# Reordering the first transfers of a retention-plus-MLP kernel: token chunks ahead of weight pieces, refills held back, more dummy matmuls

## The chip, the cores and the metric

The kernel runs on one core of one Trainium2 chip. The time is the device time of one execution in microseconds (us), the median of several executions. The profile is one execution recorded by the hardware profiler. Its engines are PE (TensorE matmul), PEld (its weight loads), DVE (VectorE), ACT (ScalarE), POOL (GpSimd) and SP (SyncE, which here issues transfers). L331 is line 331 of the kernel that was profiled, and the change and each experiment shift the lines a little: the scaling of a chunk is L331 before and L346 after. "PEclk" is the share of full speed that TensorE's clock was granted. In the profile's lines `kq` is a chunk's k and q, `am` its masked scores, and `r`, `hp` and `o` hold results of matmuls; the brackets give the engine's idle time before the line and what ended it.

## The reference

A retention layer (a linear attention with decay) is followed by an MLP with the activation h * erf(softplus(h)).

```python
for t in range(S):                                   # B=4, H=8, S=768, D=64
    state = gamma * state + k[t] (outer) v[t]
    y[t] = scale * q[t] @ state
x = y.transpose(0, 2, 1, 3).reshape(3072, 512)
h = x @ w_in                                         # 512 x 2048
out = (h * erf(softplus(h))) @ w_out                 # 2048 x 512
```

q, k and v are float32; the weights arrive as float64.

## The kernel before

The tokens are worked on in 24 chunks of 128. Chunk j needs k, q and v (256 KB each, three places in a ring of buffers). VectorE scales k and q (`K_`), TensorE transposes them (`T`), makes scores (`S_`), VectorE masks (`M`), TensorE makes outputs (`O_`) and the state's update (`U`), and VectorE adds the update to the state (`A`). The weights arrive in 16 pieces of 1 MB, p0 to p15, of which p0 to p3 are of w_in ("in") and p4, p5 of w_out ("out"). Each is read as raw 64-bit words into one of four spare places and turned into float32 by six VectorE steps and one on ScalarE (`conversion`). These steps are generators, taken one at a time by `pace`, so that they fall between the other instructions of VectorE. When a piece is converted its place is free, and the next piece for that place is loaded.

```python
def load(j):                                   # chunk j: k, q, v
    ...
    for i, src in enumerate((k, q)):
        queue = nc.scalar if i and j < 3 else nc.sync
        queue.dma_start(KQ[j][:, i], ...)
    nc.sync.dma_start(V[j], ...)

def load_pieces_after(n):                      # piece n is converted: refill its place
    for later in range(n + 1, n_p):
        if place[later] == place[n]:
            load_piece(later)
            break
...
load(0)
...
load_piece(0)
load(1)
load_piece(1)
load(2)
...
for _ in range(10):
    nc.tensor.matmul(idle, ident, ident, start=True, stop=True)
...
def ret_state(j):                              # U
    ...
    if j + 3 < NJ:
        load(j + 3)
    if j < 2:
        load_piece(j + 2)
...
for j in range(6):                             # the first six chunks, before any MLP work
    S_(j); M(j); K_(j + 1); O_(j)
    if j + 1 < 6: T(j + 1)
    U(j); pace(1)
    if j + 1 < 6: A(j)
# then hidden(0, u), u = 0..3, with chunks 6 and 7 between:
#   T(6) after u=0;  K_(7) within u=1;  S_(6), T(7) after u=1;  M(6) within u=2; ...
```

## Time and profile before

| | kernel before |
|---|---|
| median time (first three runs) | 758.63 us (758.58 to 760.79) |
| span of the profiled run | 756.3 us |
| TensorE busy | 96% |
| start of unbroken matmuls | 87.2 us |
| transfers moved from 0 to 63.46 us | 212 GB/s at a DMA share of 1.04 |

The head, some 87 us, is where TensorE waits; the remaining 669 us are matmuls back to back. The prediction below shows and reads the lines.

### The profile page before, as it was taken

The page shows a single profiled execution, that of the slowest core. Times are in us where ns is not written, and L with a number is a line of the kernel's source. Part 1 is how long each engine was busy: PE and PEld are TensorE (multiplying, and loading weights), DVE is VectorE, ACT ScalarE, POOL GpSimd, SP SyncE. Part 2 cuts the span into 40 slices and gives each one's busy share as a digit, 9 for nine tenths or more (in the row PEclk, how much of TensorE's full clock was granted, in tenths as well). Part 3 has the DMA queues.
Part 4 walks back from the last instruction along what each step waited for, and adds up shares of the span by engine and source line. Part 5 has one row for each costly group of instructions (what it writes and reads, how often), then busy time and mean ns, then how long its engine had stood idle before and what let it go on. Part 6 is the DMA issues. An engine that isn't in the chain of part 4 may idle for free.

```text
span 756.3 us, 11745 instructions
## 1 busy us (share of the span) xinstructions
PE 726.7 (96%) x5236; PEld 611.5 (81%) x5236; DVE 353.3 (47%) x463; ACT 274.8 (36%) x320; POOL 31.9 (4%) x28
## 2 busy tenths in 40 slices
PE   6857999999999999999999999999999999999997
PEld 5644444447699999999999999999999999999995
DVE  3759899985463243243153053163163152153323
ACT  2313663441524424414424424324234244324430
POOL 1000200000110110110100110101100000000000
PEclk7879999999999999999999999999999999999999
DMA  9996754202120220220220230220200000000000
GB/s 190 207 246 147 186 131 145 101 0 40 59 42 2 42 70 1 43 71 1 43 70 1 43 70 1 42 60 11 44 29 1 1 29 1 1 29 1 1 28 29
DMA packets 87522, 42.71 MB, mean 56 GB/s; under 512 B 76208, under 2 KB 76208, under 8 KB 87472
## 3 DMA queue, kind: packets, MB, share of 16 engines
q1 hardware_dynamic: 83920, 41.16, 22.9%
q10 hardware_dynamic: 3552, 0.80, 0.7%
q8 instruction: 41, 0.67, 0.4%
q14 instruction: 9, 0.07, 0.0%
HBM read 35.66 MB, written 6.29 MB: 55 GB/s over the span
## 4 chain that ended last, share of the span: by engine, by line
PE 89%; DMA 4%; DVE 3%; ACT 1%; SPq 1%; issue 1%; DVEq 0%; ACTq 0%
PE hp L536 33%; PE o L596 31%; PE o L479 7%; PE hp L466 6%; DMA kq<-in_q_dram 3%; PE r L340 2%; PE r L393 2%; PE r L353 2%; PE r L407 2%; PE r L388 1%; DMA w_in_sb<-in_moe_w_in_dram 1%; PE hp L353 1%; DVE am L365 1%; DVE kq L331 0%; DMA kq<-in_k_dram 0%
## 5 line engine op out<-in xcount | busy, mean ns | idle before, releaser
L536 PE MATMUL hp<-xs,w_in_sb 128*128 128x128 f32 x1280 | 158.7, 278 | 0.0
L536 PEld LDWEIGHTS hp<-xs,w_in_sb 128*128 128x128 f32 x1280 | 150.3, 192 | 6.7 <-issue 3.2
L596 PE MATMUL o<-w_out_sb,h 128*128 128x256 f32 x640 | 141.6, 379 | 0.0
L455 DVE TENSOR_TENSOR e<-h,e 128x1024 f32<-128x1024 f32 x44 | 51.9, 1222 | 180.1 <-ACT e L436 180.1
L596 PEld LDWEIGHTS o<-w_out_sb,h 128*128 128x128 f32 x640 | 121.6, 190 | 16.5
L536 PE MATMUL hp<-xT,w_in_sb 128*128 128x128 f32 x960 | 113.7, 275 | 0.0
L536 PEld LDWEIGHTS hp<-xT,w_in_sb 128*128 128x128 f32 x960 | 111.9, 192 | 1.9 <-issue 1.0
L596 PE MATMUL o<-w_out_sb,e 128*128 128x256 f32 x480 | 111.5, 382 | 0.9 <-DVE e L455 0.9
L596 PEld LDWEIGHTS o<-w_out_sb,e 128*128 128x128 f32 x480 | 88.1, 190 | 12.5 <-DVE e L455 1.3
L435 ACT ACT_TABLE_LOAD x24 | 30.8, 1283 | 91.1 <-PE o L596 89.1
L466 PE MATMUL hp<-xT,w_in_sb 128*128 128x512 f32 x128 | 56.9, 599 | 0.0
L564 DVE TENSOR_TENSOR h<-h,hp 128x512 f32<-128x512 f32 x20 | 13.8, 688 | 86.7 <-PE hp L536 86.7
L331 POOL TENSOR_TENSOR kq<-kq,kq_s 128x1024 f32<-128x1024 f32 x15 | 29.7, 1981 | 501.7 <-DMA kq<-in_q_dram 429.0
L466 PEld LDWEIGHTS hp<-xT,w_in_sb 128*128 128x128 f32 x128 | 24.2, 193 | 28.9 <-issue 28.2
L559 DVE TENSOR_TENSOR h<-h,hp 128x512 f32<-128x512 f32 x20 | 13.8, 688 | 71.1 <-ACT h L557 71.1
L436 ACT ACTIVATE e<-e 128x2048 f32<-128x2048 f32 x22 | 42.1, 1913 | 0.2
L435 ACT ACTIVATE e<-h 128x2048 f32<-128x2048 f32 x22 | 42.1, 1912 | 0.2
L398 ACT COPY xT<-r 128x256 f32<-128x256 f32 x42 | 13.9, 376 | 75.7 <-PE r L393 75.7
L340 PE MATMUL r<-ident,kq 128*128 128x128 f32 x168 | 24.7, 291 | 14.3 <-DVE kq L331 9.9
L562 ACT COPY h<-hp 128x512 f32<-128x512 f32 x20 | 11.7, 587 | 70.8 <-PE hp L536 70.8
L365 DVE TENSOR_TENSOR am<-r,causal 128x512 f32<-128x512 f32 x42 | 27.2, 684 | 15.8 <-PE r L353 15.8
L340 PEld LDWEIGHTS r<-ident,kq 128*128 128x128 f32 x168 | 20.6, 151 | 16.0 <-issue 9.4
(91 smaller groups left out, 688.6 us busy)
## 6 DMA issues: line engine op xcount, KB each, us to landing
w_out_sb<-in_moe_w_out_dram SPq DMA_DIRECT2D x14, 512.0 KB, 4.6
kq<-in_k_dram SPq DMA_DIRECT2D x24, 256.0 KB, 3.3
v<-in_v_dram SPq DMA_DIRECT2D x24, 256.0 KB, 4.3
w_in_sb<-in_moe_w_in_dram SPq DMA_DIRECT2D x12, 512.0 KB, 6.8
out_dram<-r SPq DMA_DIRECT2D x24, 256.0 KB, 2.3
kq<-in_q_dram SPq DMA_DIRECT2D x21, 256.0 KB, 4.1
w_out_sb<-in_moe_w_in_dram SPq DMA_DIRECT2D x4, 512.0 KB, 10.1
w_in_sb<-in_moe_w_out_dram SPq DMA_DIRECT2D x2, 512.0 KB, 4.0
```

What stands on the lines that cost most here:

```text
L331: engine.tensor_tensor(KQ[j], KQ[j], by, op=ALU.mult)
L340: nc.tensor.transpose(p[:, u, :], KQ[j][:, i, 2 * u : 2 * u + 2, :].rearrange("p h d -> p (h d)"), ident,)
L353: nc.tensor.matmul(pp[s][:, hp, :], KT[j][s * D : (s + 1) * D, hp, :], QT[j][s * D : (s + 1) * D, hp, :], start=True, stop=True,)
L365: nc.vector.tensor_tensor(AM[j][:, s], SC[j][s], causal[:, None, :].to_broadcast([P, HP, C]), op=ALU.mult)
L393: nc.tensor.matmul(place(h), V[j][:, h, :], AM[j][:, h % 2, h // 2, :], start=(not c and h % 4 < 2), stop=True, skip_group_check=True,)
L435: nc.scalar.activation(E[g], HS[g], AF.Softplus)
L436: nc.scalar.activation(E[g], E[g], AF.Erf)
L455: nc.vector.tensor_tensor(E[g][:, half], HS[g][:, half], E[g][:, half], op=ALU.mult)
L466: nc.tensor.matmul(p, w_in_of(ft, kk), XC[0][:, kk, :], start=(kk == 0), stop=(kk == n_k - 1))
L479: nc.tensor.matmul(O[0][tt].rearrange("p (d c) -> p d c", d=2), E[g][:, u * TCH + tt * P : u * TCH + (tt + 1) * P], w_out_of(ft), start=(f ...
L536: nc.tensor.matmul(bank[:, u, :], w_in_sb[:, s, IN[a], kk, u * P : (u + 1) * P], XS[m][b][:, kk, :], start=(p in (1, 2, 5) and u == 0 and ...
L596: nc.tensor.matmul(O[m][i][:, half, :], G[g][a][:, u * P : (u + 1) * P], w_out_sb[:, s, OUT[b], u, :], start=i not in started, stop=(s == ...
```

## The change

The intent is to let chunks of tokens, for which TensorE waits, arrive ahead of weights for which nothing waits yet, and to keep TensorE's clock up with dummy matmuls in the first gaps. The core of the diff:

```diff
     def load_pieces_after(n):
         for later in range(n + 1, n_p):
             if place[later] == place[n]:
-                load_piece(later)
+                if early:
+                    held.append(later)
+                else:
+                    load_piece(later)
                 break
+    def load_held():
+        for n in held:
+            load_piece(n)
+        held.clear()
...
+    load(1)
     load_piece(0)
-    load(1)
+    load(2)
     load_piece(1)
-    load(2)
...
-    for _ in range(10):
-        nc.tensor.matmul(idle, ident, ident, start=True, stop=True)
+    def keep_warm(n):
+        for _ in range(n):
+            nc.tensor.matmul(idle, ident, ident, start=True, stop=True)
+    keep_warm(16)
...
+        if j >= 4:
+            load_held()
         if j + 3 < NJ:
             load(j + 3)
-        if j < 2:
-            load_piece(j + 2)
+        if j in (1, 2):
+            load_piece(j + 1)
...
     T(0)
+    keep_warm(3)
...
         S_(j)
+        if j == 0:
+            keep_warm(3)
...
     early = False
+    load_held()
```

More of the change, by code (lines that the diff above doesn't have):

```diff
@@ L151, in load_piece @@
                 )
+    held = []
     def load_pieces_after(n):
```

## The prediction

> **What bounds the kernel now.** I read the page's slices first, to see where the TensorE (PE) is not full.
>
> ```profile
> PE   6857999999999999999999999999999999999997
> DVE  3759899985463243243153053163163152153323
> ...
> PEclk7879999999999999999999999999999999999999
> DMA  9996754202120220220220230220200000000000
> GB/s 190 207 246 147 186 131 145 101 0 40 59 42 2 42 70 1 43 71 1 43 70 1 43 70 1 42 60 11 44 29 1 1 29 1 1 29 1 1 28 29
> ```
>
> A slice is 756.3 / 40 = 18.9 us. PE is short of nine tenths in the first four slices only, some 76 us, and there the transfers are near full. Then the chain of work that ended last, in order of time: from 87.26 us on it holds matmuls almost without a break.
>
> ```profile
> 38.05 10.89 DMA kq<-in_q_dram
> 48.93 0.03 issue
> ...
> 78.58 0.71 PE r L407 x16
> ...
> 87.26 13.93 PE hp L466 x32
> 101.19 13.73 PE o L479 x32
> ```
>
> So the run is a head of 87.26 us and 756.3 - 87.26 = 669.0 us of matmuls. Nothing in the diff removes one of those, so I predict the head alone. What PE waits for there is in the timeline by engine (start, duration, instruction, in brackets the idle time before it and its releaser):
>
> ```profile
> 50.35 1.09 PE L340 MATMUL r<-ident,kq 128*128 128x128 f32 x4 [6.57 <-DVE kq L331]
> ...
> 70.78 1.97 PE L340 MATMUL r<-ident,kq 128*128 128x128 f32 x8 [4.14 <-DVE am L365]
> ```
>
> ```profile
> 49.03 1.23 DVE L331 TENSOR_TENSOR kq<-kq,kq_s 128x1024 f32<-128x1024 f32 x1 [6.18 <-DMA kq<-in_q_dram]
> ...
> 64.65 1.22 DVE L331 TENSOR_TENSOR kq<-kq,kq_s 128x1024 f32<-128x1024 f32 x1
> ```
>
> I call chunk j of k, q and v "c j", weight piece n "p n", and the VectorE (DVE) scaling of chunk j (L331) "K j". K5 idled 6.18 us for c5's q, K1 2.03 us for c1's q, K2 1.43 us for c2's k. The long PE gap at 66.6 to 70.8 us is different: T(7) waits for a mask multiply that stands behind weight conversions on DVE. Why c5 came late, the issues of the SyncE queue show:
>
> ```profile
> 33.44 1.76 SPq L138 DMA_DIRECT2D w_in_sb<-in_moe_w_in_dram  x2
> 35.29 2.20 SPq L146 DMA_DIRECT2D w_out_sb<-in_moe_w_out_dram  x2
> 37.59 0.41 SPq L95 DMA_DIRECT2D kq<-in_k_dram  x1
> 38.05 4.29 SPq L95 DMA_DIRECT2D kq<-in_q_dram  x1
> ```
>
> p3 (L138) and p4 (L146), 2 MiB together, stand ahead of c5. Yet the first conversion step of p4 ran on DVE only at 64.05 us. The windows confirm that the transfers are the limit up to about 63 us: 0.00 to 63.46 us moved 212 GB/s at a DMA share of 1.04, and only 46 to 48 us was nearly empty (85 GB/s).
>
> **What the Trainium skill says.** "DMA: Bandwidth & Descriptors", section "Issuing engines are not separate DMA queues": transfers issued from different engines run on the same 16 DMA engines and interleave. The trace agrees: c1's q, issued from ScalarE at 4.28 us, landed 10.66 us later beside p0 from SyncE, where c0's q took 4.6. So order decides, not the queue. The same page, "Why small descriptors are slow (HBM only)": a 256-byte descriptor pays a 27% overhead in the engine. The chunks move in packets of 256 bytes here; a chunk (0.79 MB) landed every 3.0 to 3.3 us, that is about 250 GB/s, while an "out" piece reached about 350 GB/s. "TensorE: Matmul & The Clock Gate", Part 1: the clock is halved by default and released after a busy window of some 3.4 us. The trace agrees: the granted clock is 0.50 from 8.6 to 22.3 us, and again from 46.2 to 56.4 and 70.1 to 73.5 us after idle stretches, the changes being multiples of 3.41 us apart. The same page, "Architectural detail": DVE is strict first-in, first-out. The trace shows DVE idle before K5 with later conversion steps of landed pieces behind it.
>
> **The change, part by part.** Bytes are unchanged up to c8; the order is not. Before: c0 p0 c1 p1 c2 c3 p2 c4 p3 p4 c5 c6 p5 c7 c8. After: c0 c1 p0 c2 p1 c3 c4 p2 c5 p3 c6 p4 p5 c7 c8. Ahead of c5, p3 and p4 go away; ahead of c6, p4; ahead of c7, nothing.
>
> Service times, from landings in the trace: chunk 3.2 us (c6 3.29, c7 2.98, c8 3.13); "in" piece 5.2 us (p2: 28.38 to 33.70); "out" piece 2.8 us (p4: 44.73 to 47.25; p5 3.96). Starting at c0's 6.4 us, the new order adds up to c1 9.6, p0 14.8, c2 18.0, p1 23.2, c3 26.4, c4 29.6, p2 34.8, c5 38.0, p3 43.2, c6 46.4, p4 49.2, p5 52.0, c7 55.2 us. The old order gives the same 55.2 us for c7, but the trace shows 60.33, so 5.1 us are lost to interleaving of two queues early and to the hole at 46 to 48 us. I let half of it return, in proportion: c5 39.6, c6 48.4, c7 57.7 us. q lands about 0.8 us ahead of v.
>
> DVE, with the spacings of the kernel before as cost. K1 starts at about 12 us, after the masks of chunk 0, instead of 15.06. The next DVE steps are p0's first conversion steps, and p0 is now later than c1: I take 16.0 us. Their 2.6 us (0.69 + 1.22 + 0.69), the state copy (0.42) and two masks (1.27) put K2 at 20.2, before 24.14. K3 follows by the old 6.87 at 27.1; K4 by 5.56 at 32.6; K5 by 6.26 (old K4 to the end of the masks of chunk 4) at 38.9, its q having landed at 38.8. K5 gains 49.03 - 38.9 = 10.1 us. K6 would follow by 7.56 at 46.5, but its q lands at 47.6: K6 47.7, before 56.59, gain 8.9. K7 follows by 8.06 at 55.8, but its q lands at 56.9: K7 57.0, before 64.65. The gain has shrunk to 7.6 us, since c7 has as many bytes ahead of it as ever.
>
> From K7 to T(7) DVE does the same steps (6.13 us), so T(7) moves from 70.78 to 63.1. From there on PE, ScalarE and DVE hand over to each other. The PE gap before T(7) grows, since PE reaches it earlier than DVE does: chunk 6's scores would end at about 56. The clock is then surely halved at T(7), and for longer than the 2.7 us of before. T(7) took 1.97 us at half speed against 1.04 for T(6); I charge 1.2 us more for this stage (an estimate: half of one further 2.4 us at half clock). Net: 7.6 - 1.2 = 6.4 us.
>
> Dummy matmuls: the first ten took 4.30 us; six more at 0.22 to 0.43 us are 1.3 to 2.6 us, ending by 6.8 to 8.3, where T(0) starts at 7.28. Three more fill the 0.73 us gap before S(0), and three the 1.31 us before O(0). They cost about nothing, at worst 1 us at T(0). They may save 1 us each on S(0), T(1), S(1), which the wait for p0 swallows. I count zero.
>
> 758.63 - 6.4 = 752.2 us.
>
> **The rivals.** First, full return: c6 and c7 land at the ideal times and DVE alone paces. DVE was busy 35.8 us between K1 and K7 (23.26 + 4.68 + 7.84, windows 15.06:49.03, 49.03:56.59, 56.59:64.65). From 12 us, with some 4 us of hand-over idling, K7 comes at 52 to 53: gain 11 to 12, less the clock, 748. Against it: c7 would need every byte ahead of it at undisturbed rates. Second, transfer-bound throughout: c7 lands at 60.3 as before. K7 at 59.7, gain 5, less the clock, 755. For it: the loaded bytes are the same, and the long issues (4.29 us) show a full queue. Third, p0 becomes the stall: with q2 interleaved it lands at 18 us, DVE stands on it and K2 gains nothing. The later chunks still gain from their order, so 753 to 756. Fourth, the held pieces starve conversions: p4 would have to land after about 57 us (K7's new time), p5 after about 65. I expect both by 55, so this is worth nothing. Beyond 87 us PE is full and every refill is released by a conversion, which moves along.
>
> **Range and chances.** The first and second rivals bound it at 748 and 755; the reported runs differ among themselves by 2 us. I take 749 to 756. Over 2% would be 15.2 us, more than DVE's own work in the head allows; slower by 2% would need a new stall of 15 us beyond the gain. So 0.98 for within 2%.
>
> **What would show it.** In the new timeline: the idle before K5 gone and K5 near 39; K6 and K7 waiting for q, if at all, by about 1 us; T(7) near 63 with a PE gap of over 6 us; p4 and p5 landed before their first steps; unbroken matmuls from about 81 us. A wait of DVE L176 on p0 near 14 to 16 us would be new. The prediction is wrong if c7 lands at 60 or later, if the matmuls after 87 us take other than 669 us, or if the clock stays full through the T(7) gap.

## The result, and the profile after

The changed kernel takes 754.58 us (median of four runs, 754.10 to 756.00); the kernel before took 759.39 us in the same rounds. The ratio is 0.9938 (95% interval 0.9916 to 0.9960). All ratios here are the mean time of one kernel's runs over that of the other's runs of the same rounds, so not quite the ratio of the medians quoted. Executions over 1.5% slower than the fastest of the same kernel are left out of the means. In five later rounds the same kernel came out at 0.9939. That is within 2%, and within the predicted range of 749 to 756 us, though 2.4 us above the predicted 752.2.

The page of the changed kernel, its 40 slices (18.8 us each now):

```profile
PE   7884999999999999999999999999999999999997
...
PEclk9997999999999999999999999999999999999999
DMA  9999755102120120120220220120200000000000
```

TensorE is still short in the first four slices. The first three together have more TensorE work than before (7, 8, 8 against 6, 8, 5), the fourth has less (4 against 7): the waiting moved to a later place. The transfers are full to the end of the fourth slice. VectorE's timeline, the scalings K5, K6 and K7 in order:

```profile
39.77 1.23 DVE L346 TENSOR_TENSOR kq<-kq,kq_s 128x1024 f32<-128x1024 f32 x1 [0.77 <-DMA kq<-in_q_dram]
...
49.93 1.22 DVE L346 TENSOR_TENSOR kq<-kq,kq_s 128x1024 f32<-128x1024 f32 x1 [3.23 <-DMA kq<-in_q_dram]
...
60.10 1.23 DVE L346 TENSOR_TENSOR kq<-kq,kq_s 128x1024 f32<-128x1024 f32 x1 [2.04 <-DMA kq<-in_q_dram]
```

The 6.18 us of idle time ahead of K5 are down to 0.77, but K6 and K7, which waited for no transfer before, now wait 3.23 and 2.04 us for theirs. K5 is 9.26 us earlier than before, K6 6.66 (it stood at 56.59), K7 4.55. The landing of c7 caps the gain. TensorE's timeline from T(7) on:

```profile
66.24 1.97 PE L355 MATMUL r<-ident,kq 128*128 128x128 f32 x8 [9.39 <-DVE am L380]
68.00 5.46 PE L483 MATMUL hp<-xT,w_in_sb 128*128 128x512 f32 x8
...
84.03 14.00 PE L483 MATMUL hp<-xT,w_in_sb 128*128 128x512 f32 x32
```

The same stretch of the kernel before, whose first line (70.78) and whose 87 us stand in the prediction, has this for the second:

```profile
72.54 4.08 PE L466 MATMUL hp<-xT,w_in_sb 128*128 128x512 f32 x8
```

T(7) came 4.54 us earlier, but its followers took longer, at a clock of 0.50 from 61.5 to 71.8 us. Unbroken matmuls start at 84.03, 3.16 us earlier than before (87.19 in the same view). After them nothing changed: 752.8 - 84.03 = 668.8 us, before 669.1. The chain that ended last, in order of time (start, duration, what), carries the transfer:

```profile
47.63 3.65 PE hp L483 x8
51.27 0.06 SPq L95
51.33 0.04 issue
51.38 8.63 DMA kq<-in_q_dram
60.01 0.03 issue
60.06 0.04 issue
60.10 1.23 DVE kq L346
```

From 51.38 to 60.01 us the end of the whole run hangs on c7's q; before, it hung on c5's q, from 38.05 to 48.93 us. (The step to TensorE just before is inferred by the profile and is not read here: SyncE issued p5 until 50.37 us and c7's k from 50.48 to 51.33, without a stop.) The profiled runs differ by 3.5 us (756.3 and 752.8), the timed ones by 4.8: the kernel before ran between 757 and 762 us over all rounds, and its profiled run (758.04) is on the quick side.

### The profile page after: what moved, and what is told of

It is laid out like the page before. It is cut to its first block, busy times and chain, and to the rows that moved or that the text cites. A ratio compares the mean times of both kernels' runs of the same rounds, so it can differ in the third digit from the quotient of the medians.

```text
span 752.8 us, 11796 instructions
## 1 busy us (share of the span) xinstructions
PE 726.2 (96%) x5260; PEld 610.7 (81%) x5260; DVE 353.2 (47%) x463; ACT 274.5 (36%) x320; POOL 32.2 (4%) x28
## 4 chain that ended last, share of the span: by engine, by line
PE 90%; DVE 4%; DMA 2%; ACT 1%; issue 1%; SPq 1%; ACTq 0%; DVEq 0%
PE hp L553 34%; PE o L613 32%; PE o L496 7%; PE hp L483 7%; PE r L408 2%; PE r L355 2%; PE r L368 2%; PE r L422 1%; DMA w_out_sb<-in_moe_w_in_dram 1%; DMA kq<-in_q_dram 1%; PE r L403 1%; DVE am L380 1%; DVE w_out_sb L191 0%; SPq L96 0%; DVE w_out_sb L201 0%
```

## The experiments

Twelve kernels ran, the two that are compared among them; every experiment's output was correct. Theory 1: K7 now waits for c7, which has the same bytes ahead of it as before the change; everything that happens to earlier chunks is hidden under that. Theory 2: VectorE's own chain bounds K7, so the order of the early chunks is what counts. Theory 3: the clock after the idle gap before T(7) takes back a part. The table has for each profiled run when c7's q landed, when K7 and T(7) began and when the unbroken matmuls began (us), then the time in rounds.

| run | c7's q | K7 | T(7) | unbroken | median | ratio (95%) |
|---|---|---|---|---|---|---|
| before | 59.46 | 64.65 | 70.78 | 87.19 | 758.6 to 759.4 | 1 |
| changed | 60.01 | 60.10 | 66.24 | 84.03 | 754.58 | 0.9938 (0.9916-0.9960) |
| after_again | 60.71 | 60.80 | 66.94 | 84.66 | 753.87 | 0.9939 (0.9920-0.9959) |
| b1_behind_c7 | 52.94 | 58.65 | 64.78 | 81.39 | 752.14 | 0.9914 (0.9901-0.9928) |
| c1_warm_gap | 60.42 | 60.52 | 66.66 | 81.94 | 751.84 | 0.9902 (0.9888-0.9915) |
| a3_no_hold | 58.64 * | 59.75 * | 65.88 * | 82.90 * | 753.83 | 0.9936 (0.9922-0.9949) |
| a4_only_hold | 59.91 | 61.27 | 67.40 | 84.33 | 754.94 | 0.9950 (0.9937-0.9962) |
| a1_no_dummies | 58.57 | 58.67 | 64.81 | 81.41 | 752.82 | 0.9919 (0.9903-0.9934) |
| a2_only_dummies | 59.91 | 65.40 | 71.53 | 89.07 | 759.74 | 1.0008 (0.9992-1.0024) |
| d1_q_on_sp | 61.36 | 61.45 | 67.59 | 85.22 | 754.34 | 0.9944 (0.9926-0.9962) |
| d2_halves | 65.23 | 65.33 | 71.46 | 88.46 | 759.24 | 1.0004 (0.9988-1.0019) |
| e1_c7_warm | 52.48 | 58.39 | 65.37 | 80.42 | 750.92 | 0.9898 (0.9884-0.9912) |
| e3_p5_behind_c7 | 55.97 | 56.95 | 65.51 | 80.54 | 750.99 | 0.9897 (0.9878-0.9915) |

\* of a3_look, the same kernel. Two sums hold all through. The span less the start of the unbroken matmuls is 668.6 to 669.1 us in every run. T(7) less K7 is 6.13 or 6.14 us in all but the last two. The median of a3_no_hold counts its slow run (below), its ratio does not. Each profile is of one execution: with the changed order of transfers (changed, after_again, c1, a1) c7's q landed anywhere from 58.57 to 60.71 us, so that a difference of under 2 us between two profiles is not by itself an effect.

**b1_behind_c7.** Takes bytes away from ahead of c7: theory 1 against 2.

```diff
-        if j >= 4:
-            load_held()
         if j + 3 < NJ:
             load(j + 3)
+        if j >= 4:
+            load_held()
```

> Edit: the two held pieces p4 and p5 are issued behind chunk 7 instead of behind chunk 6. Theory 1 (after the change the scaling K7 waits for chunk 7, because the same bytes lie ahead of it as before the change): q of chunk 7 lands about 5 us earlier, near 55 us; K7 no longer waits for it but follows the conversions, at K6 + 8.06 = 58.0 us instead of 60.10; T(7) near 64.1 instead of 66.24; the time falls by about 2 us against the changed kernel (to 752.5). Rival theory 2 (VectorE's own chain bounds K7 and the wait is incidental): K7 stays at 60 and the time at 754.5. Rival 3 (p4 then lands too late for its first conversion step, which stands ahead of K7 on VectorE): K7 at 60 or later, time 754.5 to 756.

VectorE's lines up to K7, then TensorE's T(7) and the start of the unbroken matmuls:

```profile
58.03 0.69 DVE L187 TENSOR_SCALAR w_out_sb<-w_out_sb 128x1024 uint32<-128x1024 uint32 x1 [1.18 <-DMA w_out_sb<-in_moe_w_out_dram]
58.65 1.22 DVE L346 TENSOR_TENSOR kq<-kq,kq_s 128x1024 f32<-128x1024 f32 x1
```

```profile
64.78 1.97 PE L355 MATMUL r<-ident,kq 128*128 128x128 f32 x8 [8.54 <-DVE am L380]
66.54 4.30 PE L483 MATMUL hp<-xT,w_in_sb 128*128 128x512 f32 x8
```

c7's q landed 7 us earlier, K7 no longer waits for it, and the ratio fell from 0.9938 to 0.9914, 1.8 us (the intervals overlap a little). In all six runs with p4 and p5 ahead of c7 and K7 bound by it (changed, after_again, c1, a1, d1, d2) K7 begins 0.09 or 0.10 us after that landing; here it does not. So theory 1 holds for the wait. K7's 1.45 us alone would not show it, since a1 has K7 at 58.67 without this edit; e3 below is clearer. And of the 2.64 us at the unbroken matmuls only 1.46 are T(7)'s; 1.18 come from a stretch behind T(7) that the clock made shorter. The rival of a late p4 is there too, at 1.18 us: VectorE takes its instructions in order, and p4's first step stands just ahead of K7. K7 moved by 1.45 us of the 2.1 expected.

**c1_warm_gap.** Keeps the clock up: theory 3.

```diff
-            ([(S_, 6), (T, 7)], [(M, 6)]),
+            ([(S_, 6), (keep_warm, 40), (T, 7)], [(M, 6)]),
```

> Edit: 40 dummy matmuls (0.215 us each at full clock, 8.6 us) between the scores of chunk 6 and T(7), in the 9.39 us for which TensorE idles. Theory (the growth of this gap from 4.14 to 9.39 us cost 1.4 us of the gain, since the clock stayed halved until 71.8 us instead of 73.5 - 70.1 = 3.4 us): the granted clock stays 1.0 through the gap, T(7) takes about 1.1 us instead of 1.97 and the eight matmuls of the next group 3.6 instead of 5.46 us; unbroken matmuls start 2.5 us earlier, near 81.5 instead of 84.1; the time falls by 2 to 2.7 us against the changed kernel, to about 752. Rival (from T(7) on VectorE paces, not TensorE): the durations shorten but the start of the unbroken matmuls stays near 84 and the time within 0.5 us.

```profile
66.66 1.26 PE L355 MATMUL r<-ident,kq 128*128 128x128 f32 x8 [0.17 <-DVE am L380]
67.75 3.60 PE L483 MATMUL hp<-xT,w_in_sb 128*128 128x512 f32 x8
...
81.94 10.57 PE L483 MATMUL hp<-xT,w_in_sb 128*128 128x512 f32 x24
```

(The count of the last line is cut by the view's end.) T(7) began 0.42 us later than in the changed kernel, the unbroken matmuls 2.09 us earlier: the stretch between took 15.28 us instead of 17.79. The timed gain over the changed kernel is 0.9938 - 0.9902, that is 2.7 us. TensorE, not VectorE, paces that stretch, and the clock costs 2.5 us there. That this cost comes from the growth of the gap, as the expectation says, does not hold, though. The stretch took 16.41 us in the kernel before, 17.54 in a2_only_dummies and 16.93 in a4_only_hold, all three with a gap of 4.14 us, and 16.60 in a1_no_dummies with a gap of 7.62. With gaps from 4.14 to 9.7 us it lies between 16.4 and 17.8 in no order; with the gap filled it is 15.0 to 15.3. What it costs goes with how long the clock stays halved after T(7) has begun: 2.72 us in the kernel before, 3.17 in b1_behind_c7, 5.52 in the changed kernel. Over the ten profiles of the table without the 40 dummies the stretch is 15.03 us (that of e3, all at full clock) plus half of this time, to within 0.02 us in nine of them and 0.20 in a4_only_hold.

**a3_no_hold** and **a4_only_hold** undo one half of the reordering each.

```diff
 # a3: the changed kernel, refills at once again
-                if early:
-                    held.append(later)
-                else:
-                    load_piece(later)
+                load_piece(later)
 # a4: the changed kernel, first pieces ahead of their chunks again
-    load(1)
     load_piece(0)
-    load(2)
+    load(1)
     load_piece(1)
+    load(2)
...
-        if j in (1, 2):
-            load_piece(j + 1)
+        if j < 2:
+            load_piece(j + 2)
```

> Edit: the changed kernel with freed places refilled at once again (p4 goes ahead of chunk 5, p5 ahead of chunk 7). Theory 1: chunk 7 has the same bytes ahead of it, so its q lands near 60 again; chunk 5 about 2.8 us later (K5 near 42.5), chunk 6 as in the kernel before (q near 52.5), K7 at K6 + 8.06 = 60.6; T(7) near 66.8; time within 1 us of the changed kernel (754.5 to 755.5): the hold alone is worth almost nothing. Rival (the hold is what made the gain): time back to about 758.

> Edit: the hold and the dummies of the changed kernel, but the pieces p0 to p3 ahead of their chunks as in the kernel before. Theory 1: chunk 5 has p4 no more ahead of it, so K5 near 46.5; K6 at K5 + 7.56 = 54; K7 at K6 + 8.06 = 62.1; about 2.5 us faster than the kernel before at K7, less about 1 us for the halved clock: 756.5 to 757.5. Rival (the hold is the whole gain): 754.5. Second rival (early chunks' order is the whole gain): 759.

One of a3's timed runs, the profiled one, fell into a state with a granted clock of about 0.65 and took 1056.7 us; it is not read, and a3_look gave the profile.

> The kernel without the hold again, for a profile: the one of its timed runs fell into a state with a clock of 0.66 and a time of 1057 us and is not read. Expected as before: q of chunk 7 near 60, K5 near 42.5 to 45, K6 near 52.5, K7 60 to 61; time near 754.

VectorE's K5, K6 and K7 in a3_look:

```profile
43.46 1.23 DVE L343 TENSOR_TENSOR kq<-kq,kq_s 128x1024 f32<-128x1024 f32 x1 [4.70 <-DMA kq<-in_q_dram]
...
51.69 1.23 DVE L343 TENSOR_TENSOR kq<-kq,kq_s 128x1024 f32<-128x1024 f32 x1 [0.71 <-DMA kq<-in_q_dram]
...
59.75 1.22 DVE L343 TENSOR_TENSOR kq<-kq,kq_s 128x1024 f32<-128x1024 f32 x1
```

K5 is 3.7 us later than with the hold, K7 no later. The time is the same (0.9936 against 0.9938). For a4 the steps came as expected (K5 46.38 for 46.5, K6 53.22 for 54, K7 61.27 for 62.1), but the time is 754.94, 1.6 us below the expected 756.5 to 757.5. Two parts can be read: K7 came 0.8 us earlier than expected, and the halved clock took back 0.52 us (a stretch of 16.93 against 16.41) instead of 1. In the profiled runs the unbroken matmuls of a4 start only 0.30 us after those of the changed kernel. So either half of the reordering brings nearly the whole gain, and the two together hardly more. Theory 1 alone does not say why: in neither run does K7 wait for c7's q, which had landed 1.11 and 1.36 us before it. K7 follows VectorE's own steps, 8.06 and 8.05 us after K6 as in the kernel before, and K6 or K5 had waited for a transfer. The two bounds of K7, c7's landing and VectorE's chain from K6, lie close together here, and both are near 60 us.

**a1_no_dummies** and **a2_only_dummies** take the dummies away and take them alone (10 at the start, or 16 and twice 3).

```diff
 # a1: the changed kernel
-    keep_warm(16)
+    keep_warm(10)
     T(0)
-    keep_warm(3)
...
-        if j == 0:
-            keep_warm(3)
 # a2: the kernel before with the three keep_warm calls of the change
```

> Edit: the changed kernel with the dummy matmuls of the kernel before (10 at the start, none around the first scores). Theory (worth zero, since the early chunks' path ends in waits for transfers): K5, K6 and K7 still wait for their q; K7 near 60.1; time 754 to 755, within 0.5 us of the changed kernel. Rival (they carry part of the gain): the clock is halved from 8.6 to 22 us as before, K2 and K3 come 1 to 2 us later and the time is 755.5 to 757.

> Edit: the kernel before with the dummy matmuls of the change alone. Theory: the clock is full through the first chunks but K1, K2 and K5 wait for the same transfers, so K5 near 49, T(7) near 70.8, time 758 to 759.5. Rival (the clock carries the gain): 755 to 757.

Alone they bring nothing (1.0008): K5 still waited 5.02 us for its transfer. Without them the kernel came out faster, not slower, at 0.9919.

> The changed kernel as it is, again, in five rounds. The run without its dummy matmuls came out at 0.9919 of the kernel before (0.9903 to 0.9934), the changed kernel at 0.9938 (0.9916 to 0.996), with q of chunk 7 at 58.57 against 60.01 us. If the dummies cost something: again 0.993 to 0.994 and q of chunk 7 near 60. If the difference was between chips or runs: 0.992 or below, with q of chunk 7 between 58.5 and 60.

It gave 0.9939 (0.9920 to 0.9959), which overlaps the interval without dummies (0.9903 to 0.9934). By medians the dummies would cost 1 us. c7's q landed at 60.71 with them and 58.57 without, but it landed at 58.64 in a3_look, which has them (and another order of pieces). Whether they cost anything stays open; they do not help.

The run without them holds a second lesson. K1, VectorE's scaling of chunk 1:

```profile
16.07 1.23 DVE L346 TENSOR_TENSOR kq<-kq,kq_s 128x1024 f32<-128x1024 f32 x1 [2.69 <-issue]
```

In the changed kernel K1 stands at 11.86. Here c1's q landed at 15.99 us instead of 10.65, behind p0, although the program puts it ahead: ScalarE's queue issues it, and did so only when c0's q had landed (issue at 6.76 us after a landing at 6.74; in the changed kernel 5.69 after 5.67), and by then p0 was issued. Yet K7 came earlier than in the changed kernel. Four microseconds at chunk 1 vanish in the later waits.

**d1_q_on_sp** and **d2_halves** ask why c7 landed 5 us later than the sum of service times.

```diff
 # d1
-            queue = nc.scalar if i and j < 3 else nc.sync
+            queue = nc.sync
 # d2: each "in" piece is two transfers of 64 partitions
-                nc.sync.dma_start(
+                (nc.gpsimd if r and n < 4 else nc.sync).dma_start(
```

> Edit: the q of chunks 0 to 2 issued from SyncE as all others, so that one queue carries all of it and chunk 1 lands whole ahead of p0. In two runs q of chunk 1, issued from ScalarE behind a wait, fell behind p0 and landed near 16 us, in three near 10.6. Theory 1: K1 near 12 us, K7 still at the landing of q of chunk 7, 58.5 to 60; time within 1 us of the changed kernel. Rival (the 5.1 us that the sum of service times fell short of the measured landing of chunk 7 were lost to two queues interleaving): chunk 7's q near 57, time 2 to 3 us less. Rival 2 (SyncE's own issues become the limit early): c0 and K0 about 1 us later, time up to 1 us more.

> Edit: of the first four pieces (all of w_in, two transfers of 64 partitions each) the second half is issued from GpSimd, so that both halves are under way together. An in piece took 5.2 to 5.8 us, an out piece of the same bytes and packets (128 partitions) about 2.8. If the 64 partitions are what slows it: an in piece takes about 3 us, chunk 7's q lands some 4 x 2.2 = 9 us earlier, K5 to K7 follow VectorE's own chain (K7 near 54) and the time falls to 749 to 751. Rival (the rows of w_in in memory, or the sum of the bytes, sets the rate): an in piece as before, q of chunk 7 near 60, time 754 to 755.5. Rival 2 (GpSimd's issuing is slow or in the way of its scale multiplies): p0 later than 15.6, time 756 or more.

(The "three near 10.6" of the first expectation landed at 10.65, 12.29 and 13.06 us.) With one queue c1 lands whole ahead of p0 and K1 stands at 11.46, but c7's q lands at 61.36, not 57: the interleaving of two queues was not what cost 5 us.

d2 did not do what it was meant to do. GpSimd issued its halves of p0 and p1 at 1.51 and 2.29 us, ahead of chunks, and SyncE the other halves only at 6.50 and 17.17 us. The two halves of p0 were under way together for 4.4 us, those of p1 not at all (the first had landed at 13.13). p0 was complete at 20.22 us. The decay factors landed at 13.46 us instead of 7.93, and ScalarE stood 8.7 us in the issue of c2's q, waiting for an earlier transfer, so that chunk 0's scores began only at 16.38 us; c7's q came at 65.23. p0 and the time are as the second rival has them. The sum of bytes came no faster: at 34.14 us four chunks and 3 MB of pieces had landed; in the kernel before the same amount had landed at 33.70. Whether the 64 partitions make an "in" piece slow is not tested by this run, in which each of its transfers still fills 64 partitions; that rival stands.

**e1_c7_warm** and **e3_p5_behind_c7** combine.

```diff
 # e1: the edits of b1 and c1 together
 # e3: c1, and p4 ahead of chunk 7 but p5 behind it
-        if j >= 4:
-            load_held()
+        if j == 4:
+            load_held(1)                       # only the first held piece
         if j + 3 < NJ:
             load(j + 3)
+        if j >= 4:
+            load_held()
```

> Edit: both at once, p4 and p5 behind chunk 7 and 40 dummy matmuls ahead of T(7). Alone they moved the start of the unbroken matmuls from 84.10 to 81.39 and to 81.94 us. If the transfers and the clock are two separate terms of one path, as theory 1 has it: T(7) near 64.8, then 15.3 us as in the run with the dummies alone, unbroken matmuls from about 80.1 us, time about 750.2. Rival (the dummies delay T(7): 8.6 us of them from 56.2 end at 64.9, just when T(7) becomes free): up to 0.5 us worse. Rival 2 (the two overlap, b1's gain being the clock's phase alone): 752.

> Edit: p4 ahead of chunk 7 as in the change, p5 behind it, and the 40 dummy matmuls ahead of T(7). With both pieces behind chunk 7, VectorE waited 1.2 us for p4 just ahead of K7. Here p4 lands about 2.8 us after chunk 6, near 52, and q of chunk 7 near 56, both before VectorE asks for them. So K7 at K6 + 8.06 = 57 to 57.5 us, T(7) near 63.3, unbroken matmuls near 79.0; time about 749.5 to 750, 1 us below the run with both behind. Rival (the dummies now end at 65 and hold T(7) back): T(7) at 65, time 751.

e3's K7 and T(7):

```profile
56.95 1.22 DVE L346 TENSOR_TENSOR kq<-kq,kq_s 128x1024 f32<-128x1024 f32 x1
```

```profile
65.51 1.04 PE L355 MATMUL r<-ident,kq 128*128 128x128 f32 x8
```

K7 is where it was expected (57 to 57.5), waiting for neither p4 nor c7. This is the clearest sign for theory 1, as the earliest K7 with both pieces ahead of c7 was 58.67 us. But T(7) comes 8.56 us after it, not 6.13: the rival is right, the 40 dummies, begun at 56.47 us, took 9.20 us and hold T(7) back. In e1 they did so by 0.85 us (6.98), and the two gains did not add: its unbroken matmuls begin 3.61 us before those of the changed kernel, where b1 and c1 had 2.64 and 2.09, since a part of b1's was the clock's. Both beat the kernel before and the changed kernel, at 0.9898 and 0.9897 of the kernel before (750.9 and 751.0 us); their intervals do not tell them from c1 alone. With 30 dummies e3 should save some 2 us more (an estimate: at 0.23 us each they would end at 63.4, where T(7) began at 65.51); it was not run.

## Why the prediction was right or wrong

The range held the time, and the choice of within 2% was right. But the prediction had named "if c7 lands at 60 or later" as a sign that it is wrong, and c7's q landed at 60.01 us and its v at 60.82. T(7) came at 66.24 for "near 63", the unbroken matmuls at 84.03 for "about 81", and K6 and K7 waited 3.23 and 2.04 us for q instead of "about 1". The range held because it took in the second rival (755), not because the main reckoning was right. Two of SyncE's issues in the changed kernel, of c6's v and of p4 and p5, bear on the third step below:

```profile
41.35 6.64 SPq L96 DMA_DIRECT2D v<-in_v_dram  x1
48.09 2.29 SPq L146 DMA_DIRECT2D w_out_sb<-in_moe_w_out_dram  x4
```

By its steps:

- **The head alone counts: right.** The matmuls after it took 668.6 to 669.1 us in all thirteen profiled runs of the table.
- **VectorE's chain up to K5: right.** p0's first step was predicted at 16.0 and came at 15.64; K2 20.2 and 19.77; K3 27.1 and 27.16; K4 32.6 and 32.73; K5 38.9 and 39.77 us. (This is one profile: K1, 11.86 here, stood anywhere from 11.46 to 16.07 in the others that have c1 ahead of p0, d2 aside.)
- **"I let half of it return, in proportion: c5 39.6, c6 48.4, c7 57.7 us": this step failed.** c5's q landed at 39.68 for a predicted 38.8, but c6's at 49.84 for 47.6 and c7's at 60.01 for 56.9. At c7 nothing of the 5.1 us came back. So K7's gain was 4.55 us, not 7.6. Against the bare sum c7 was 5.6 us late (60.82 for 55.2). By landings of the last part of each, 2.7 of them had gathered by p2 (37.52 for 34.8), in small parts over chunks and pieces. c5 took 5.7 us (37.52 to 43.20) against 3.2, of which c6 gave back 0.85 (2.35 against 3.2). p4 and p5 took 4.36 and 3.25 (50.70 to 58.31) against 2.8 each, and c7 gave back 0.7. The 2.8 was too small from the start: the kernel before has 2.52 for p4 and the 3.96 for p5 that the prediction itself quotes. From 46 to 50 us only 150 GB/s moved, while SyncE was still in the issue of c6's v (6.64 us, until 47.99) and came to p4 only at 48.09 (the two lines above). The kernel before has the same picture at 46 to 48 us, at 85 GB/s. That the long issue makes the hole was argued, not shown; d1 only excludes the interleaving of two queues, and why the terms were larger stays open.
- **The mechanism is the second rival's:** "transfer-bound throughout: c7 lands at 60.3 as before", with a gain of 5 us, less the clock. b1 and e3 show it from the other side: fewer bytes ahead of c7, and K7 no longer waits for it (58.65 and 56.95). VectorE's chain from K6 is the next bound and lies close, as a3 and a4 show.
- **The clock's 1.2 us: right in form and size (1.38), by luck.** The clock stayed halved after T(7) for 2.80 us more than before (5.52 for 2.72), for a predicted 2.4, and half of that is what it cost. But the experiments show no link to the gap's length, the reason that the prediction gives: in a1_no_dummies, with a gap of 7.62 us, it was 0.42 us more and cost 0.19. Against the 15.28 us of c1, the halved clock costs 1.1 us in the kernel before and 2.5 in the changed one; that difference goes with how long the halved clock lasts after T(7), not with how long TensorE had idled. The clock's recorded changes are multiples of 3.41 us apart in every profile but that of the slow run, so it may be chance where T(7) falls between two of them; no run shows this. (The prediction's list of halved stretches leaves out the one from 25.71 to 29.12 us.)
- **Dummies count zero: right, as far as it was tested** (a2). Early chunks also count nothing by themselves: with K1 at 16.07 the gain was no smaller.
- **Held pieces starve nothing: right here, and close.** p4 landed at 55.06, its first step ran at 57.38; p5 landed at 58.31 for an expected 55, its first step ran at 67.84. Put behind c7 (b1), p4 was waited for, 1.18 us.
- **The net:** predicted 7.6 - 1.2 = 6.4; the profiled runs have 4.54 - 1.38 = 3.16 at the unbroken matmuls and 3.5 in the span; the timed runs 4.8.

## What to carry to other kernels

When transfers are the limit, a new order brings forward only those that get fewer bytes ahead of them: here c5's q landed 9.25 us earlier and c7's no earlier (60.01 for 59.46). Sum the bytes ahead of the last transfer that the chain waits for, because a gain at an earlier one is lost there, and look how far behind it the next bound lies. Look for what is behind the critical wait on an in-order engine before a transfer is put off: the next step in its line may need it. And once a kernel waits, the waits give room for work that keeps the clock up, but it must end before the awaited work is ready.

## What the Trainium skill lacked or had wrong

- "DMA: Bandwidth & Descriptors", section "Issuing engines are not separate DMA queues", calls the issue time usually small relative to the transfer. Here the issue of one 256 KB transfer on SyncE took from 0.37 to 6.64 us; the longest was most of the 9.35 us from its start to its landing, and p4's issue came only after it.
- "TensorE: Matmul & The Clock Gate", Part 1, gives a busy window of about 3.4 us for the return of the full clock. It is not wrong, but not to be taken as the wait for full speed: in the changed kernel matmuls resumed at 66.24 us and the clock was halved until 71.76, 5.5 us later; in the kernel before from 70.78 to 73.50, 2.7 us. The page's free-running window allows for both.
- No page has a state for a program on one core like that of one run of a3_no_hold: a granted clock of about 0.65 and 1056.7 instead of 754 us.
